# A gelu that writes back into its PSUM bank, and a reordered opening, in a fused linear-attention and mixer-MLP kernel

## The chip, the core and the metric

The kernel runs on one core of one Trainium2 chip. The metric is the device time of one execution in microseconds (us), and lower is better. The five engines are named as in the profile: PE (matrix multiply; PEld is its weight load), DVE (vector), ACT (scalar, activations), POOL (GpSimd) and SP, whose queue issues nearly all DMAs.

## What is computed

The reference, cut to what matters. The sequence has S = 2048 tokens, the model width is D = 640, the hidden width F = 1728, and there are 32 heads of 20.

```python
xn = layernorm(x)
q, k, v = split_heads(xn @ wqkv)
pq, pk = q @ w_phi, k @ w_phi                      # per head
phi_q = concat([softmax(pq), softmax(-pq)])        # the feature maps
phi_k = concat([softmax(pk), softmax(-pk)])
o = (phi_q @ (phi_k.T @ v)) / (phi_q @ phi_k.T @ 1 + 1e-6)
h = gelu(layernorm(xn) @ w1 + b1)                  # the channel-mixing MLP
out = x + o @ wo + (h @ w2 + b2)
```

## The kernel before, in words

Float32 products are made from exact splits: `split` writes a rounded copy `hi` (ACT, L61) and the rest `lo` (a subtraction on DVE or POOL, L64), and `mm3` (L70 to L72) adds three products, hi by hi, hi by lo and lo by hi. Tokens stand in four blocks of 512 (b = 0 to 3), F in 14 chunks of 128 (c), taken in pairs (group g, member j). Model width is contracted in five steps (kc).

**Order.** In the opening and in the MLP of blocks 0 and 1, instructions of PE, DVE, ACT and POOL stand on their queues in the order in which the code calls them. Steps that run beside the products hang on a generator, `mlp.beside`; `tick()` is called after each `mm3` step and moves that generator to its next `yield`. Between the MLP of blocks 0 and 1 and the second half of the kernel only PE's order is the code's; DVE, ACT, POOL and, throughout, SP's DMA queue are ordered by the scheduler when the program is built. An engine runs its queue strictly in order, and so does SP.

**Opening.** PE runs 18 warm-up products (L579). `stats` (L138 to L162) makes each token's mean and scale, `centre` (L166) and `scale` (L170, L172) normalise token tiles x0[0] to x0[3] in place, one on DVE and one on ACT of each pair. `make_y0` (L174) transposes a pair of tiles on PE (L181) into PSUM banks, in pieces of 2, 2 and 1 of the five kc blocks, and `split` turns each piece into y[0] hi (ACT) and lo (DVE). `half_first` (L542) then makes the hidden products of chunks 0 and 1 for that half of the tokens (30 products of 256 columns, L549). PSUM tiles come from `Banks`, which hands out the eight banks by the list given to it; `pall` is the list of the opening. The gelu of these four results (`zs`) is called later, from `next_y` (L652).

**First pass and second pass of the MLP.** `Mlp.first` (L273) makes a hidden product of 128 by 512 in a bank of `self.ph` (banks 0, 1, 2 in turn) and calls `Mlp.gelu` (L281): ACT reads the bank, adds the bias and writes gelu to the SBUF tile `gt` (L286), ACT copies `gt` to hi, DVE subtracts for lo. So the bank is free again as soon as ACT has read it. `passes` (L289) calls `first` for j = 0 and 1 and then makes five second products m = 0 to 4 in banks 5, 6, 7 (`self.po`), each added to the accumulator by DVE (L329, L331). A hidden tile of (g, j, b) = (0, 0, 2) is first copied to `gt` by DVE (L284).

**`next_y`** runs beside group 0 and 1 of block 0: `rows` (L187) sends means and scales through a PE transpose (L197) and DRAM and back as a broadcast tile `m` (L202, L207); the gelu of `zs`; the splits of the w2 halves of chunks 2 and 3 (`parts[c][1]()`: ACT copy, POOL subtraction); after four ticks the subtraction on the feature maps' weights `wpt` (L669, DVE), which products L646 read later; nine ticks on, normalising block 1 into y[1] (L677 POOL, L679 DVE, L681 ACT, L683 DVE).

**The join in the middle.** After the attention projections (L906, L976) come the first passes of group 0 for blocks 2 and 3: first product (0,2) j = 0 and j = 1, the last key-value product (L976, L980), then (0,3) j = 0 and j = 1, at 431 to 446 us. `mlp.ph` is there the same turn of banks 0, 1, 2 as the projections use. At this time DVE transposes the last query features (L1003), SP stores them (L1009: sixteen DMAs of 160 KB), loads t-combinations of y into y[3] (L1345: four DMAs of 256 KB), weights (L354, L356) and the first features back for the attention (L1176, L1178). The products of `cross` (L395) read these y[3] tiles.

Of the kernel before, what the change touches and what calls it, by code (L numbers as in the profile page):

```python
# [10 lines left out]
AF = mybir.ActivationFunctionType  # L11
# [4 lines left out]
P = 128  # L16
# [35 lines left out]
def tile_kernel(ctx: ExitStack, tc: tile.TileContext, x, xT, wkT, wqT, wv, wphi, wo, w1, b1, w2, b2,  # L52
# [4 lines left out]
    def split(hi, lo, src, scale=None, eng=nc.vector, first=nc.scalar):  # L57

        if scale is None:
            if first is nc.scalar:  # L60
                nc.scalar.activation(hi, src, AF.Copy)  # L61
            else:
                first.tensor_copy(hi, src)
            eng.tensor_tensor(lo, src, f(hi), op=ALU.subtract)  # L64
        else:
            nc.scalar.activation(hi, src, AF.Copy, scale=scale)
            nc.vector.scalar_tensor_tensor(lo, src, scale, f(hi), op0=ALU.mult, op1=ALU.subtract)
# [100 lines left out]
    def scale(t, xb, act=False):  # L168
        if act:
            nc.scalar.activation(xb, xb, AF.Copy, scale=ry[:, t:t + 1])  # L170
        else:
            nc.vector.tensor_scalar_mul(xb, xb, ry[:, t:t + 1])  # L172

    def make_y0(half, xbs, ptile):  # L174

        cols = slice(half * 256, half * 256 + 256)
        for c0, n in ((0, 2), (2, 2), (4, 1)):
            ps = ptile()
            for c in range(n):
                for i in range(2):  # L180
                    nc.tensor.transpose(ps[:, c * 256 + i * P:c * 256 + (i + 1) * P],  # L181
                                        xbs[i][:, (c0 + c) * P:(c0 + c + 1) * P], idt)
            src = ps[:, :n * 256].rearrange("p (c t) -> p c t", c=n)
            cs = slice(c0, c0 + n)
            split(y[0][0][:, cs, cols], y[0][1][:, cs, cols], src)
            yield
# [27 lines left out]
    class Mlp:  # L214
# [67 lines left out]
        def gelu(self, g, j, pz, gt, hh, hl, out=False):  # L282
            if out:
                nc.vector.tensor_copy(gt, pz)  # L284
                pz = gt
            nc.scalar.activation(gt, pz, AF.Gelu_apprx_tanh, bias=b1t[:, 2 * g + j:2 * g + j + 1])  # L286
            split(hh, hl, gt)

        def passes(self, g, b, ws, hid=None):  # L289

# [243 lines left out]
    nc.scalar.dma_start(b1t, b1)  # L534
    nc.scalar.dma_start(b2t, b2)
    y[0], y[1] = ([yp.tile([P, KC, 512], F32R, name=f"y{p}{b}") for p in range(2)] for b in range(2))
    gts = mtile(4)
    hid = [mtile(2 * j + 1, F32R) for j in range(2)]
    hid = [(h[:, 0, :512], h[:, 1, :512]) for h in hid]
    pall = Banks(5, 6, 7, 3, 4, 0, 1, 5, 2, 6)  # L540
# [1 line left out]
    def half_first(half, *order):  # L542

        cols = slice(half * 256, half * 256 + 256)
        pz = [pall()[:, cols] for _ in range(2)]
        last = {op[0]: op for op in order}
        for j, wi, yi in order:
            for kc in range(KC):
                nc.tensor.matmul(pz[j], wc[j][wi][:, kc, :], y[0][yi][:, kc, cols],  # L549
                                 start=(wi, yi, kc) == (0, 0, 0), stop=kc == KC - 1 and last[j] == (j, wi, yi))  # L550
        return [lambda j=j: mlp.gelu(0, j, pz[j], *[m[:, cols] for m in (gts[:, j, :512], *hid[j])]) for j in range(2)]

    x1 = load_x(range(4, 8), xp)
    for c, pool in ((2, None), (3, r0)):
# [27 lines left out]
    centre(0, x0[0])  # L582
    step(s01, 3)
    centre(1, x0[1])
    scale(0, x0[0])
    scale(1, x0[1], True)
    parts[0][0]()
    step(s23, 2)
    y01, y23 = make_y0(0, x0[:2], pall), make_y0(1, x0[2:], pall)
# [3 lines left out]
    step(s23, 1)  # L593
    centre(2, x0[2])
    centre(3, x0[3])
    scale(2, x0[2])
    scale(3, x0[3], True)
    zs = half_first(0, *((j, wi, yi) for j in range(2) for wi, yi in ((0, 0), (1 - j, j), (j, 1 - j))))
    parts[2][0]()
    step(s47, 2)  # L600
    step(y23, 4)
    zs += half_first(1, *((j, wi, yi) for ops in (((0, 0), (1, 0)), ((0, 1),)) for j in range(2) for wi, yi in ops))
    parts[3][0]()
    step(s47, 2)
    step(s01, 1)
    step(s47, 1)
    step(s47, 1)
    rows1 = rows(1, 1, xp, Banks(3), 1, nc.scalar)
    next(rows1)
    for c in range(2):  # L610
        parts[c][1](nc.vector)
# [41 lines left out]
    def next_y():  # L653

        for _ in range(3):
            yield
        next(rows1)
        for z in zs[:2]:
            z()
        finish(rows1)  # L660
        mr = load_rows(1)
        first_raws.extend(raws(jobs[0]))
        for z in zs[2:]:
            z()
        for c in range(2, 4):
            parts[c][1]()
        for _ in range(4):
            yield
        nc.vector.tensor_tensor(wpt[:, :, :, 1:], wpt[:, :, :, 1:], wpt[:, :, :, 0:1].to_broadcast([G6, 6, 6, DF]), op=ALU.subtract)  # L669
        for _ in range(9):  # L670
            yield
        xcs = {}
        for n in range(2 * KC + 5):
            c, i = divmod(n, 2)
            if i == 0 and c < KC:
                xcs[c] = xp.tile([P, D], F32, name="xb")[:, :512]
                nc.gpsimd.tensor_tensor(xcs[c], acc[1][:, c], mr[:, 0], op=ALU.subtract)  # L677
            if i == 0 and 0 <= (d := c - 1) < KC:
                nc.vector.tensor_tensor(xcs[d], xcs[d], mr[:, 1], op=ALU.mult)  # L679
            if i == 1 and 0 <= (d := c - 1) < KC:  # L680
                nc.scalar.activation(y[1][0][:, d], xcs[d], AF.Copy)  # L681
            if i == 0 and 0 <= (d := c - 2) < KC:
                nc.vector.tensor_tensor(y[1][1][:, d], xcs[d], f(y[1][0][:, d]), op=ALU.subtract)  # L683
            yield
        for st in (s23, s47):
            step(st, 1)
            yield
# [924 lines left out]
```

## Time and profile before

| | before |
|---|---|
| runs, us | 709.28, 710.75, 711.32; median 710.75 |
| the profiled execution, us | 709.75 |
| its span, us | 708.0 |
| PE busy | 701.1 (99%) |
| DVE, ACT, POOL busy | 526.4, 353.1, 435.6 |
| granted PE clock | 0.999 |
| DMA moved | 107.61 MB, mean 152 GB/s |

A row of the timeline has start, duration (both us), engine, line, operation, out<-in, form and count; in brackets the idle time before it and what ended it. The list of waits has engine, tile and line, what was waited for, then total us, times and longest us. Rows of a tile give the shortest, median and longest duration in ns. "SPq" is an issue on SP's queue: its duration is the issue, not the transfer.

### The profile page before, as it was taken

The numbers are of one execution on the slowest core, as the hardware profiler recorded it, in microseconds if no ns is written. First come the engines' busy times: TensorE is split into PE (matmuls) and PEld (weight loads), VectorE is DVE, ScalarE is ACT, GpSimd is POOL, SyncE is SP. The second block draws the span as 40 slices with busy tenths as digits, with TensorE's granted clock in tenths as the row PEclk, the third lists the DMA queues.
The fourth block names the chain that finished last, engine by engine and source line by source line (L and its number), as shares of the span: only waits on it lengthen the run. The fifth ranks groups of instructions, "written<-read, shape, count | busy, mean of one in ns | idle before, by whom it ended". The sixth has DMA issues, their size and how long they took to land.

```text
span 708.0 us, 9794 instructions
## 1 busy us (share of the span) xinstructions
PE 701.1 (99%) x3369; PEld 590.3 (83%) x3369; DVE 526.4 (74%) x840; ACT 353.1 (50%) x583; POOL 435.6 (62%) x374
## 2 busy tenths in 40 slices
PE   9999999999999999999999999999999999999998
PEld 7788888888888888888888888878888878888886
DVE  7877755988745788788888878748678785696773
ACT  6434554444434545544444547457676757561250
POOL 3611314577245997898777979548688897462530
PEclk9999999999999999999999999999999999999999
DMA  9823642475621227336400708873355558537212
GB/s 328 287 74 113 190 122 98 156 263 174 219 105 74 94 75 231 86 97 200 114 0 15 177 0 316 227 215 126 109 160 172 164 166 276 216 124 262 91 60 104
DMA packets 66295, 107.61 MB, mean 152 GB/s; under 512 B 7478, under 2 KB 31830, under 8 KB 64366
## 3 DMA queue, kind: packets, MB, share of 16 engines
q1 hardware_dynamic: 65942, 106.98, 47.1%
q8 instruction: 26, 0.43, 0.2%
q14 instruction: 23, 0.19, 0.1%
q10 hardware_dynamic: 304, 0.01, 0.0%
HBM read 72.42 MB, written 34.55 MB: 151 GB/s over the span
## 4 chain that ended last, share of the span: by engine, by line
PE 93%; DVE 4%; ACT 1%; DMA 1%; issue 0%; ACTq 0%; DVEq 0%; SPq 0%
PE bank L906 28%; PE bank L70 18%; PE bank L72 18%; PE bank L71 18%; PE bank L976 3%; PE bank L646 2%; PE bank L1214 1%; PE bank L1215 1%; DVE st L138 1%; DMA e<-e 1%; PE bank L308 1%; PE bank L327 1%; PE bank L326 1%; PE bank L307 1%; PE bank L1146 1%
## 5 line engine op out<-in xcount | busy, mean ns | idle before, releaser
L906 PE MATMUL bank<-wkh,y 128*128 128x512 f32 (+1 forms) x480 | 139.6, 365 | 0.0
L64 POOL TENSOR_TENSOR w<-r,w 128x640 fp32r<-128x640 f32 x32 | 52.3, 1648 | 93.1 <-ACT w L61 57.7
L70 PE MATMUL bank<-m,w 128*128 128x512 f32 x274 | 108.0, 394 | 1.1 <-DVE acc L329 1.0
L71 PE MATMUL bank<-m,w 128*128 128x512 f32 x274 | 106.8, 390 | 0.0
L70 PE MATMUL bank<-y,w 128*128 128x512 f32 (+1 forms) x274 | 106.5, 389 | 0.0
L71 PE MATMUL bank<-y,w 128*128 128x512 f32 (+1 forms) x274 | 106.1, 387 | 0.0
L72 PE MATMUL bank<-y,w 128*128 128x512 f32 (+1 forms) x270 | 104.4, 387 | 0.0
L72 PE MATMUL bank<-m,w 128*128 128x512 f32 x262 | 102.1, 390 | 0.0
L906 PEld LDWEIGHTS bank<-wkh,y 128*128 128x128 f32 x480 | 87.6, 188 | 13.2
L906 PE MATMUL bank<-wkl,y 128*128 128x512 f32 (+1 forms) x240 | 87.4, 364 | 0.0
L942 ACT ACTIVATE m<-m,rs_all 128x1280 f32<-128x1280 f32 x32 | 43.7, 1365 | 42.9 <-POOL m L941 42.8
L70 PEld LDWEIGHTS bank<-m,w 128*128 128x128 f32 x274 | 51.5, 188 | 12.4 <-DVE acc L329 1.4
L70 PEld LDWEIGHTS bank<-y,w 128*128 128x128 f32 x274 | 51.5, 188 | 10.8 <-issue 0.4
L71 PEld LDWEIGHTS bank<-y,w 128*128 128x128 f32 x274 | 51.5, 188 | 10.5 <-DMA y<-t 0.4
L71 PEld LDWEIGHTS bank<-m,w 128*128 128x128 f32 x274 | 51.5, 188 | 10.4 <-DVE m L461 0.2
L72 PEld LDWEIGHTS bank<-y,w 128*128 128x128 f32 x270 | 50.8, 188 | 10.3
L944 DVE TENSOR_REDUCE sm<-m 128x64 f32<-128x1280 f32 x32 | 47.4, 1482 | 14.9 <-ACT m L942 14.8
L72 PEld LDWEIGHTS bank<-m,w 128*128 128x128 f32 x262 | 49.2, 188 | 10.3
L906 PE MATMUL bank<-w,y 128*128 128x512 f32 x240 | 57.4, 391 | 0.0
L941 POOL TENSOR_TENSOR m<-m,mx 128x640 f32<-128x640 f32 (+2 forms) x48 | 44.4, 938 | 19.3 <-DVE mx L930 19.3
L331 DVE TENSOR_TENSOR acc<-bank,acc 128x512 f32<-128x512 f32 x70 | 47.0, 684 | 11.0 <-PE bank L72 6.1
L64 DVE TENSOR_TENSOR m<-m,m 128x512 fp32r<-128x512 f32 (+1 forms) x34 | 27.9, 828 | 36.0 <-ACT m L61 36.0
(216 smaller groups left out, 1516.7 us busy)
## 6 DMA issues: line engine op xcount, KB each, us to landing
r<-in_w SPq DMA_DIRECT2D x52, 320.0 KB
e<-e SPq DMA_DIRECT2D x40, 256.0 KB
e<-acc SPq DMA_DIRECT2D x52, 160.0 KB
acc<-in_xT SPq DMA_DIRECT2D x4, 1280.0 KB
t<-t SPq DMA_DIRECT2D x8, 512.0 KB
tf<-t SPq DMA_DIRECT2D x2, 1536.0 KB
xb<-in_x SPq DMA_DIRECT2D x8, 320.0 KB
t<-in_x SPq DMA_DIRECT2D x8, 320.0 KB
```

Source lines behind the costliest of these rows:

```text
L64: eng.tensor_tensor(lo, src, f(hi), op=ALU.subtract)
L70: nc.tensor.matmul(ps, lh, rh, start=first, stop=False, **kw)
L71: nc.tensor.matmul(ps, lh, rl, start=False, stop=False, **kw)
L72: nc.tensor.matmul(ps, ll, rh, start=False, stop=last, **kw)
L138: nc.vector.bn_stats(st[:, i, h, :], xb[:, h * 320:(h + 1) * 320])
L331: nc.vector.tensor_tensor(acc[b][:, m, :], pw, acc[b][:, m, :], op=ALU.add)
L646: nc.tensor.matmul(ps[:, u * nh * DF:(u + 1) * nh * DF], raw[:nh * DH, u * P:(u + 1) * P], wpt[:nh * DH, g, :nh, 1:], start=True, stop=True)
L906: nc.tensor.matmul(ps, lh[:, kc, c], rh[:, kc], start=n == 0, stop=n == 3 * KC - 1)
L941: subs[n, t] = nc.gpsimd.tensor_tensor(ep[:, s], a, b, op=ALU.subtract)
L942: exps[n, t] = nc.scalar.activation(e, e, AF.Exp, scale=rs_all[:, t:t + 1])
L944: nc.vector.tensor_reduce(sm, e.rearrange("p s (h f) -> p (s h) f", f=DH), axis=AX, op=ALU.add)
L976: nc.tensor.matmul(kvp[g // 2][:, (g % 2) * 240:(g % 2) * 240 + 240].rearrange("p (s f) -> p s f", s=4), v[:, g * VS:(g + 1) * VS], ft[:, ...
```

## The change

It has five parts.

1. `Mlp.gelu` writes gelu back into the PSUM bank (`pz`), and both parts of the split read it there. `gt` stays in use for (0, 0, 2), where `pz` is `gt`, and for (6, 1). The opening's `gts` tile goes.
2. `scale_pair`: the second tile of a pair is scaled on ACT for its first three kc blocks and on DVE for the last two.
3. `make_y0` transposes and splits in pieces of 1, 2, 2 blocks.
4. The second `half_first` runs over kc outside, chunks and weight parts inside. The first keeps its order. `rows1` takes bank 7 in place of bank 3.
5. In `next_y` the w2 half of chunk 2 gets its hi from DVE, the `wpt` subtraction follows at once, and chunk 3's w2 half comes seven ticks later; the total of ticks is unchanged.

```diff
+    def scale_pair(t):
+        scale(t, x0[t])
+        scale(t + 1, x0[t + 1][:, :3 * P], True)
+        scale(t + 1, x0[t + 1][:, 3 * P:])
+
     def make_y0(half, xbs, ptile):
-        for c0, n in ((0, 2), (2, 2), (4, 1)):
+        for c0, n in ((0, 1), (1, 2), (3, 2)):
...
-            nc.scalar.activation(gt, pz, AF.Gelu_apprx_tanh, bias=b1t[:, 2 * g + j:2 * g + j + 1])
-            split(hh, hl, gt)
+            nc.scalar.activation(pz, pz, AF.Gelu_apprx_tanh, bias=b1t[:, 2 * g + j:2 * g + j + 1])
+            split(hh, hl, pz)
...
-        for j, wi, yi in order:
-            for kc in range(KC):
-                nc.tensor.matmul(pz[j], wc[j][wi][:, kc, :], y[0][yi][:, kc, cols],
-                                 start=(wi, yi, kc) == (0, 0, 0), stop=kc == KC - 1 and last[j] == (j, wi, yi))
+        for op in order:
+            j, wi, yi, kc = op
+            nc.tensor.matmul(pz[j], wc[j][wi][:, kc, :], y[0][yi][:, kc, cols], start=(wi, yi, kc) == (0, 0, 0), stop=last[j] == op)
...
-    scale(0, x0[0])
-    scale(1, x0[1], True)
+    scale_pair(0)
...
-    scale(2, x0[2])
-    scale(3, x0[3], True)
-    zs = half_first(0, *((j, wi, yi) for j in range(2) for wi, yi in ((0, 0), (1 - j, j), (j, 1 - j))))
+    scale_pair(2)
+    zs = half_first(0, *((j, wi, yi, kc) for j in range(2) for wi, yi in ((0, 0), (1 - j, j), (j, 1 - j)) for kc in range(KC)))
...
-    zs += half_first(1, *((j, wi, yi) for ops in (((0, 0), (1, 0)), ((0, 1),)) for j in range(2) for wi, yi in ops))
+    zs += half_first(1, *((j, wi, 0, kc) for kc in range(KC) for j in range(2) for wi in range(2)),
+                     *((j, 0, 1, kc) for j in range(2) for kc in range(KC)))
...
-    rows1 = rows(1, 1, xp, Banks(3), 1, nc.scalar)
+    rows1 = rows(1, 1, xp, Banks(7), 1, nc.scalar)
...
-        for c in range(2, 4):
-            parts[c][1]()
-        for _ in range(4):
-            yield
+        parts[2][1](nc.vector)
         nc.vector.tensor_tensor(wpt[:, :, :, 1:], wpt[:, :, :, 1:], wpt[:, :, :, 0:1].to_broadcast([G6, 6, 6, DF]), op=ALU.subtract)
-        for _ in range(9):
+        for _ in range(7):
+            yield
+        parts[3][1]()
+        for _ in range(6):
             yield
```

Three places show what this does to the queues. Line numbers of the changed kernel are 2 to 5 higher.

**DVE in the opening**, from the rows' copy to the first second-pass addition. Before (`m` are SBUF tiles of the hidden layer, `w` weights, `bank` PSUM):

```order
L199 COPY sr_406<-bank_404 8x128
L64 TENSOR_TENSOR m_150<-m_149,m_150 128x256
L64 TENSOR_TENSOR m_151<-m_149,m_151 128x256
L64 TENSOR_TENSOR m_150<-m_149,m_150 128x256
L64 TENSOR_TENSOR m_151<-m_149,m_151 128x256
L64 TENSOR_TENSOR m_390<-m_389,m_390 128x512
L669 TENSOR_TENSOR wpt<-wpt 120x36x19
L64 TENSOR_TENSOR m_438<-m_389,m_438 128x512
L329 SCALAR_TENSOR_TENSOR acc_103<-bank_459,b2t,acc_103 128x512
```

The same stretch of DVE in the changed kernel:

```order
L204 COPY sr_407<-bank_405 8x128
L64 TENSOR_TENSOR m_149<-bank_265,m_149 128x256
L64 TENSOR_TENSOR m_150<-bank_266,m_150 128x256
L64 TENSOR_TENSOR m_149<-bank_325,m_149 128x256
L64 TENSOR_TENSOR m_150<-bank_326,m_150 128x256
L63 CAST w_173<-r_160 128x640
L668 TENSOR_TENSOR wpt<-wpt 120x36x19
L64 TENSOR_TENSOR m_391<-bank_392,m_391 128x512
L64 TENSOR_TENSOR m_438<-bank_439,m_438 128x512
L334 SCALAR_TENSOR_TENSOR acc_103<-bank_458,b2t,acc_103 128x512
```

The `wpt` subtraction moved ahead of both 512-column subtractions, the w2 copy of chunk 2 is new on DVE, and each L64 has now one operand in PSUM.

**DVE at the join in the middle**, around the subtraction for the hidden tile (0,2) j = 1, `m3`. Before:

```order
L1003 STREAM_TRANSPOSE acc1_2045<-m1_3995 128x10x32 x2
L1003 STREAM_TRANSPOSE et_2046<-m1_3995 128x10x32
L1003 STREAM_TRANSPOSE acc0_2044<-m1_3995 128x10x32
L64 TENSOR_TENSOR m3_4161<-m4_4139,m3_4161 128x512
L1119 COPY kxs_4204<-kxa_2031 123x160
```

And in the changed kernel, with the bank's number in the name (`bank2`):

```order
L1005 STREAM_TRANSPOSE acc1_2046<-m1_3996 128x10x32 x2
L1005 STREAM_TRANSPOSE et_2047<-m1_3996 128x10x32
L1005 STREAM_TRANSPOSE acc0_2045<-m1_3996 128x10x32
L64 TENSOR_TENSOR m3_4162<-bank2_4163,m3_4162 128x512
L1121 COPY kxs_4205<-kxa_2032 123x160
```

No row moved; the subtraction now reads bank 2 itself. The next user of bank 2 on PE's queue is the first product of (0,3) j = 1, `bank2_4241` (`bank2_4240` before).

**SP's queue at the join.** Before, from the weights' load to the first feature load (`e_73` is the store of the features of block 3, `y` the tiles of y[3], `t` the combinations in DRAM):

```order
L356 DMA r_4112<-in_w 128x640
L1345 DMA y_3061<-t_86 128x512
L1345 DMA y_3060<-t_86 128x512
L1009 DMA e_73<-acc_2045 32x10x128 x8
L1009 DMA e_73<-et 32x10x128 x4
L1009 DMA e_73<-acc_2044 32x10x128 x4
L1345 DMA y_3060<-t_87 128x512
L1345 DMA y_3061<-t_87 128x512
L354 DMA r_4367<-in_w 128x640
L354 DMA r_4368<-in_w 128x640
L1176 DMA e<-e_70 80x512
```

The changed kernel:

```order
L361 DMA r_4113<-in_w 128x640
L1011 DMA e_73<-acc_2046 32x10x128 x8
L1011 DMA e_73<-et 32x10x128 x4
L1011 DMA e_73<-acc_2045 32x10x128 x4
L1347 DMA y_3061<-t_86 128x512
L1347 DMA y_3062<-t_86 128x512
L1347 DMA y_3061<-t_87 128x512
L1347 DMA y_3062<-t_87 128x512
L359 DMA r_4368<-in_w 128x640
L359 DMA r_4369<-in_w 128x640
L1178 DMA e<-e_70 80x512
```

The first two y loads moved from ahead of the sixteen feature stores to behind them. Apart from the operands, ACT's queue differs at the join by one swap (the first copy L392 of the next weights now stands ahead of the hi copy of (0,3) j = 1) and in the opening by the w2 copies named above; POOL's queue has the same rows in the same order.

## Prediction on record

> **What bounds the kernel now.** I read the page first, then the list of waits of PE's weight loads, then the timelines of the places that it names.
>
> ```profile
> span 708.0 us, 9794 instructions
> ...
> PE   9999999999999999999999999999999999999998
> ...
> PEclk9999999999999999999999999999999999999999
> ```
>
> PE is busy in every slice at full clock. The change alters no product of PE, so it can only move PE's idle time. Because the ends of matmuls are modelled, the idle time is read from the weight loads; these rows hold most of it beside the start, which is not touched (waited-for us in total, times, longest):
>
> ```profile
> PEld bank L70 <- DVE acc L329: 1.4, 1, 1.4
> ...
> PEld bank L549 <- ACT y L61: 0.9, 4, 0.3
> PEld bank L70 <- ACT m L449: 0.7, 1, 0.7
> ...
> PEld bank L71 <- DMA y<-t: 0.4, 1, 0.4
> ```
>
> The waits for L329 and for y at L549 are what the opening's parts can take away, and the last two lie behind the join in the middle. Everything that the change could win lies in about 2.5 us, 0.35% of the time; what it could lose is not bounded by this list.
>
> **The opening, first term.** The weight loads of the opening, then ACT:
>
> ```profile
> 9.64 0.30 PEld L549 LDWEIGHTS bank<-y,w 128*128 128x128 f32 x2 [0.27 <-ACT y L61]
> 10.13 3.45 PEld L549 LDWEIGHTS bank<-y,w 128*128 128x128 f32 x28 [0.19 <-ACT y L61]
> 13.83 1.17 PEld L181 LDWEIGHTS bank<-idt,xb 128*128 128x128 f32 x10 [0.25 <-issue]
> 15.26 0.30 PEld L549 LDWEIGHTS bank<-y,w 128*128 128x128 f32 x2 [0.27 <-ACT y L61]
> 15.75 3.45 PEld L549 LDWEIGHTS bank<-y,w 128*128 128x128 f32 x28 [0.19 <-ACT y L61]
> ```
>
> ```profile
> 7.29 0.83 ACT L170 ACTIVATE xb<-xb,ry 128x640 f32<-128x640 f32 x1 [0.17 <-DVE ry L158]
> 8.99 1.36 ACT L61 ACTIVATE y<-bank 128x512 fp32r<-128x512 f32 x3 [0.24 <-PE bank L181]
> ```
>
> 28 loads in 3.45 us are 0.123 us each, so a kc block lasts 0.123 us in the first half, where ACT makes one in about 0.27 (1.36 / 5). The first half keeps its order and stays bound by ACT's five blocks. In the second half four products use one block, 0.49 us, so ACT keeps ahead, and the first piece is one block, ready before the ten transposes end: 0.27 + 0.19 = **0.46 us** go. Ahead of it, ACT scales 384 columns in place of 640: at most 0.83 x 256/640 = 0.33 us less, at least nothing; I take 0.2, since short instructions cost more per column. DVE pays with one more scaling, and then this pair decides:
>
> ```profile
> 11.50 1.16 DVE L153 TENSOR_TENSOR rr<-rr,q 128x4 f32<-128x4 f32 x1
> ```
>
> ```profile
> 11.06 1.58 POOL L64 TENSOR_TENSOR w<-r,w 128x640 fp32r<-128x640 f32 x1
> ```
>
> DVE's tiny product ended at 12.66, POOL's subtraction at 12.64: DVE was held by POOL, which started after ACT's copy. So ACT's 0.2 us come through to the scaling of tiles 2 and 3, and the second half starts 0.2 us sooner (of the 0.25 idle at 13.83). The extra DVE scaling is hidden in that hold; if the hold were gone it would cost its 0.2 to 0.3 us. First term: 0.66 us, between 0.2 and 0.9.
>
> **The opening, second term.** The wait for L329:
>
> ```profile
> 27.45 1.89 DVE L64 TENSOR_TENSOR m<-m,m 128x512 fp32r<-128x512 f32 x1 [1.62 <-ACT m L61]
> 29.27 0.86 DVE L669 TENSOR_TENSOR wpt<-wpt 120x684 f32<-120x684 f32 x1
> 30.05 0.68 DVE L64 TENSOR_TENSOR m<-m,m 128x512 fp32r<-128x512 f32 x1
> 30.65 2.05 DVE L329 SCALAR_TENSOR_TENSOR acc<-bank,b2t,acc 128x512 f32<-128x512 f32 x3
> ```
>
> ```profile
> 30.08 0.39 PE L72 MATMUL bank<-m,w 128*128 128x512 f32 x1
> 31.45 0.50 PE L70 MATMUL bank<-m,w 128*128 128x512 f32 x1 [0.98 <-DVE acc L329]
> ```
>
> ```profile
> 24.51 0.42 ACT L61 ACTIVATE m<-m 128x256 fp32r<-128x256 f32 x1
> 24.83 1.35 ACT L61 ACTIVATE w<-r 128x640 fp32r<-128x640 f32 x2
> ```
>
> ```profile
> 20.84 0.89 DVE L63 CAST w<-r 128x640 fp32r<-128x640 f32 x2
> ```
>
> PE's step is 0.23 us here, so L70 was due at 30.31 and lost 1.14. The chain behind it is the L64 of 1.89 us (the same form takes 0.68 two rows on; POOL was subtracting weights beside the long one), then `wpt`, then the next L64. In the changed kernel the last short hi copy still ends at 24.93; DVE's subtraction for it (0.4) and the new cast (0.45) bring `wpt` to 25.8, with chunk 2's copy gone from ACT and chunk 3's later. `wpt` ends at 26.66. ACT, without the 1.35 us, makes both gelus and hi copies (some 0.65 each) by 27.4, the second gelu being ready to start when its product ends near 25.5. So the first L64 runs at 26.6, the second at 27.4 to 28.1, and the first L329 ends at 28.7; PE wants the bank at 30.31 - 0.66 = 29.65. 1.14 us go, with 0.95 to spare.
>
> What PSUM as source costs is seen in two rows of the subtraction's line (ns, shortest, median, longest):
>
> ```profile
> L64 DVE TENSOR_TENSOR m<-m,m x34: 412/693/1891, 22.5 to 628.1; 128x512 fp32r<-128x512 f32 x30, 128x256 fp32r<-128x256 f32 x4
> L64 DVE TENSOR_TENSOR y<-bank,y x6: 416/637/682, 9.7 to 16.8; 128x512 fp32r<-128x512 f32 x4, 128x256 fp32r<-128x256 f32 x2
> ```
>
> The form with a bank is no longer, and never reached 1.89. [...]
>
> **What is late next** is the normalising of block 1:
>
> ```profile
> 30.70 7.19 POOL L677 TENSOR_TENSOR xb<-acc,m 128x512 f32<-128x512 f32 x5 [1.91 <-DMA m<-r]
> ```
>
> ```profile
> 38.36 0.68 DVE L331 TENSOR_TENSOR acc<-bank,acc 128x512 f32<-128x512 f32 x1
> ```
>
> ```profile
> 39.20 0.47 PE L70 MATMUL bank<-m,w 128*128 128x512 f32 x1
> ```
>
> POOL's start hangs on a DMA round trip that the change doesn't shorten (ACT issues it after the table load at the same time), and DVE's normalising steps wait for POOL block by block. PE, 1.8 us ahead, is due at 37.40 in the bank that L331 frees. By DVE's order L331 moves only from 38.36 to about 37.0 and ends near 37.7, so about 0.35 us come back (nothing to 0.6). The opening wins 0.66 + 1.14 - 0.35 = **1.45 us**, between 0.8 and 2.1.
>
> Between 43 and 431 us the other engines wait for PE, and PE for almost nothing; I carry the gain through and cost the PSUM gelu there at nothing, since three banks turn and a bank is wanted again, at the soonest, two products (30 steps of 0.23 us, 6.8 us) after its own ended.
>
> **The join: a wait added.** There this cover is missing, because the key-value product takes one of the three banks. (0,2) j = 1 and (0,3) j = 1 both have bank 2.
>
> ```profile
> 442.75 0.39 PE L70 MATMUL bank<-y,w 128*128 128x512 f32 x1
> ```
>
> ```profile
> 442.43 0.64 ACT L61 ACTIVATE m<-m 128x512 fp32r<-128x512 f32 x1
> ```
>
> ```profile
> 443.49 0.89 DVE L1003 STREAM_TRANSPOSE acc<-m 128x320 f32<-128x320 f32 x2
> ...
> 445.09 0.64 DVE L64 TENSOR_TENSOR m<-m,m 128x512 fp32r<-128x512 f32 x1
> ```
>
> PE began (0,3) j = 1 at 442.75; the gelu had read the bank by then. Now the bank is free only when DVE's subtraction ends, which stands behind four transposes on DVE: 445.73. The wait costs 445.80 - 442.75 = **3.05 us**. Behind this matmul queue all of PE's later products; DVE's transposes don't depend on them. If DVE came to the subtraction right after the hi copy (443.07), the wait would be 1.0: those are the ends.
>
> **And SP.** The y loads now follow the sixteen stores:
>
> ```profile
> 446.33 5.20 SPq L1009 DMA_DIRECT2D e<-acc  x8
> ...
> 458.59 1.44 SPq L1345 DMA_DIRECT2D y<-t  x2
> ...
> 461.38 0.36 SPq L1176 DMA_DIRECT2D e<-e  x1
> ```
>
> ```profile
> 463.94 0.19 PEld L71 LDWEIGHTS bank<-y,w 128*128 128x128 f32 x1 [0.38 <-DMA y<-t]
> ...
> 469.04 0.19 PEld L70 LDWEIGHTS bank<-tf,w 128*128 128x128 f32 x1 [0.70 <-ACT m L449]
> ```
>
> ```profile
> DMA packets 1043, 2.00 MB, mean 266 GB/s; under 512 B 127, under 2 KB 138, under 8 KB 1042
> ```
>
> The last row is of 460.4 to 467.9 us, with the DMA engines busy throughout. Two more loads, 0.52 MB, ahead of the fourth y and of the first features take 0.52 / 266 GB/s = 2.0 us. PE already waited there, 0.38 for y and 0.70 behind a feature load (ACT's copy L449 stood behind it). PE comes 3.05 late: it needs y at 463.56 + 3.05 = 466.6, and y lands at 465.9, so the 0.38 go; the features let it on at 469.04 + 2.0 = 471.0, and PE is there at 469.04 - 0.70 - 0.38 + 3.05 = 471.0. The two losses overlap: 3.05 - 0.38 - 0.70 = 1.97, and by the DMAs 2.0. I take **2.0 us**, between 1.5 (1.0 of bank wait, DMAs faster) and 3.05 (nothing overlaps).
>
> **Sum.** -1.45 + 2.0 = +0.55 us. The profiled execution took 709.75, 1.0 less than the median of the runs, 710.75; it becomes 710.3, and the median **711.3**. From the terms' bounds, -0.6 to +2.3.
>
> **Rivals.**
> *The loss doesn't overlap: slower.* The feature loads come later than 471.0, the point from which they decide. For it: the sixteen stores, 2.6 MB, were issued in the 12.3 us from 446.33 to 458.59; at that rate the 0.52 MB take 2.5 us, and SP's two more issues (1.44 by the row of 458.59) come ahead of L1176, of which I add 1.1, the rest lying beside the transfers: 3.6. Net 3.6 - 1.45 = +2.15: 712.9, and more with an opening that wins less. Against it: the y rows are longer than the stores' and ran at 266.
> *The bank wait is short: faster.* DVE takes the subtraction early (wait 1.0) and the loads run in the idle DMA time: loss 0.5, opening 2.0: 709.25.
> *The opening gives back.* `wpt` and POOL's subtraction for chunk 2 become ready together near 25.8; if POOL goes first, DVE is held as in the 1.89 us row, L329 ends at 30.1 and 0.6 us come back: 711.9. [...]
> *It doesn't do what it says*: the waits for y at L549 stay, since ACT and not the order sets them: +0.46, 711.8.
>
> **Chances.** The forecast 0.5, slower 0.2, faster 0.13, the two last together 0.17. The range, 709.4 to 713.3, reaches from the short bank wait to just beyond the slower rival and includes the spread of the runs. A measurement of this kernel tells about 0.3% (2.1 us) from no change. Only the slower rival crosses it on that side (0.2), and for the other side hardly 2 us are to be had: 0.05; within it, 0.75.
>
> **What would show it.** In the changed profile: no 0.27 and 0.19 in the second half of L549, and L70 following 30 x 0.123 = 3.7 us after the transposes' end; no wait for L329 near 30; PE 1.2 to 1.7 us ahead at the first product of block 1 (42.95 before); one PE wait of about 3 us on DVE m L64 near 441; no wait for y<-t; at 475 us a lag of about 0.5 us. I am wrong if that bank wait is missing, or if the lag there is under -0.6 or over 2.3.

## The result, and the profile after

| | before | changed |
|---|---|---|
| median of the runs beside each other, us | 710.12 (709.28 to 711.32) | 713.10 (711.92 to 714.34) |
| ratio, 95% interval | | 1.0038 (1.0026 to 1.0051) |
| the profiled execution, us | 709.75 | 711.92 |
| its span, us | 708.0 | 710.1 |

The change costs 2.7 us, from 1.8 to 3.6 by the interval. The forecast was +0.55 us (711.3), with a range up to 713.3: the time lies inside, near its upper end, and the loss is a little over the 0.3% that a measurement of this kernel can tell from no change (the six runs of before spread over 0.29%). The profiled executions differ by 2.17 us. In the groups further below two executions, of 773.76 us (granted clock 0.851) and of 3448.28 us, lie far from all others and are left out of ratios and counts.

The page of the changed kernel, in the same slices as before (1/40 of the span each, 17.75 us):

```profile
span 710.1 us, 9795 instructions
...
PE   8999999999999999999999999899999999999998
...
PEclk9999999999999999999999999999999999999999
```

Two digits of PE fell to 8. In the first slice the weight loads of the warm-up products were done sooner (5.31 us in place of 6.78) and PE stood 1.35 us for the first tile, with no loss: its transposes began at 7.96 (8.13 before). The other slice, from 444 to 461.5 us, is the join. The waits of PE's weight loads say for what (total us, times, longest):

```profile
PEld bank L70 <- DVE m L64: 3.3, 1, 3.3
...
PEld bank L70 <- DVE acc L334: 1.1, 1, 1.1
PEld bank L70 <- DVE acc L336: 0.9, 2, 0.8
...
PEld bank L553 <- ACT y L61: 0.5, 2, 0.3
...
PEld bank L553 <- DVE y L64: 0.3, 1, 0.3
```

The first row is new and longer than all that the opening lost before. The two waits for L329 (now L334) and for y at L549 (now L553) only shrank, and one for L336 came up. To see when time was won and lost I paired each PE product with the same one of before and took the difference of their starts ("PE's offset", minus means ahead):

| product that before began at, us | 16.5 | 31.6 | 43 | 442 | 447 | 475 | last, 708 |
|---|---|---|---|---|---|---|---|
| offset of the changed kernel, us | -0.64 | -0.98 | -0.12 | -0.02 | +3.16 | +2.33 | +2.17 |

**Opening.** PE's weight loads of the second half, after the transposes:

```profile
13.78 1.12 PEld L186 LDWEIGHTS bank<-idt,xb 128*128 128x128 f32 x10
14.87 3.69 PEld L553 LDWEIGHTS bank<-y,w 128*128 128x128 f32 x30
```

Thirty loads in one row without a bracket: PE waits for no block of y. But then DVE:

```profile
27.68 0.87 DVE L668 TENSOR_TENSOR wpt<-wpt 120x684 f32<-120x684 f32 x1 [2.10 <-DMA wpt<-in_wphi]
28.47 1.28 DVE L64 TENSOR_TENSOR m<-bank,m 128x512 fp32r<-128x512 f32 x2
```

The 1.89 us subtraction of before is gone (two take 1.28), but DVE stood 2.10 us for the load of `wpt`, with both of them queued behind. And the normalising of block 1, on POOL, began 1.19 us later than before (31.89 against 30.70):

```profile
31.89 1.29 POOL L679 TENSOR_TENSOR xb<-acc,m 128x512 f32<-128x512 f32 x1 [1.91 <-DMA m<-r]
```

What PE felt of the two, at the first and the fourth second-pass group:

```profile
30.46 0.50 PE L70 MATMUL bank<-m,w 128*128 128x512 f32 x1 [0.64 <-DVE acc L334]
...
39.04 0.50 PE L70 MATMUL bank<-m,w 128*128 128x512 f32 x1 [0.57 <-DVE acc L336]
```

These stood at 31.45 and 39.20 before: the lead goes from 0.99 to 0.16.

**Join.** PE, then DVE:

```profile
442.50 0.39 PE L72 MATMUL bank<-y,w 128*128 128x512 f32 x1
445.78 0.50 PE L70 MATMUL bank<-y,w 128*128 128x512 f32 x1 [2.89 <-DVE m L64]
```

```profile
443.48 0.89 DVE L1005 STREAM_TRANSPOSE acc<-m 128x320 f32<-128x320 f32 x2
444.30 0.46 DVE L1005 STREAM_TRANSPOSE et<-m 128x320 f32<-128x320 f32 x1
444.69 0.46 DVE L1005 STREAM_TRANSPOSE acc<-m 128x320 f32<-128x320 f32 x1
445.08 0.65 DVE L64 TENSOR_TENSOR m<-bank,m 128x512 fp32r<-128x512 f32 x1
```

The four transposes stand ahead of the subtraction that frees the bank, and PE starts as it ends: 445.78, forecast 445.80. SP, and ACT at the first feature tile:

```profile
457.56 2.43 SPq L1347 DMA_DIRECT2D y<-t  x4
...
461.32 0.36 SPq L1178 DMA_DIRECT2D e<-e  x1
```

```profile
468.20 0.63 ACT L1209 ACTIVATE m<-e 128x512 fp32r<-128x512 f32 x1
```

ACT no longer waits for the features, and PE's waits for y (0.38) and behind L449 (0.70) are gone: PE is so late that both are there. So the offset falls by 0.83, from +3.16 to +2.33.

### The profile page after: what moved, and what is told of

It is laid out like the page before. It is cut to its first block, busy times and chain, and to the rows that moved or that the text cites. A ratio compares the mean times of both kernels' runs of the same rounds, so it can differ in the third digit from the quotient of the medians.

```text
span 710.1 us, 9795 instructions
## 1 busy us (share of the span) xinstructions
PE 699.4 (98%) x3369; PEld 589.0 (83%) x3369; DVE 522.2 (74%) x843; ACT 350.3 (49%) x582; POOL 434.7 (61%) x374
## 4 chain that ended last, share of the span: by engine, by line
PE 85%; DVE 6%; POOL 3%; DMA 2%; ACT 2%; issue 1%; SPq 0%; POOLq 0%; DVEq 0%
PE bank L908 23%; PE bank L70 18%; PE bank L71 17%; PE bank L72 17%; PE bank L978 2%; PE bank L648 2%; POOL m L943 2%; PE bank L1216 1%; PE bank L1217 1%; DVE st L138 1%; POOL m L954 1%; DMA m<-r 1%; DMA r<-sr 1%; PE bank L312 1%; PE bank L331 1%
## 5 line engine op out<-in xcount | busy, mean ns | idle before, releaser
L64 POOL TENSOR_TENSOR w<-r,w 128x640 fp32r<-128x640 f32 x32 | 52.7, 1659 | 93.8 <-ACT w L61 63.5
L336 DVE TENSOR_TENSOR acc<-bank,acc 128x512 f32<-128x512 f32 x70 | 47.2, 684 | 12.2 <-PE bank L72 6.9
L908 PEld LDWEIGHTS bank<-w,y 128*128 128x128 f32 x240 | 44.4, 188 | 8.5
```

The costliest lines, as they stand in the source:

```text
L336: nc.vector.tensor_tensor(acc[b][:, m, :], pw, acc[b][:, m, :], op=ALU.add)
L908: nc.tensor.matmul(ps, lh[:, kc, c], rh[:, kc], start=n == 0, stop=n == 3 * KC - 1)
```

## The experiments

All comparisons stand beside runs of the kernel before in the same group. Offsets are those of the profiled execution; POOL is the start of the first subtraction of block 1.

| kernel | median, us | ratio (95%) | at 31.6 | at 43 | at 442 | at 475 | wait at the join | POOL |
|---|---|---|---|---|---|---|---|---|
| changed | 713.10 | 1.0038 (1.0026 to 1.0051) | -0.98 | -0.12 | -0.02 | +2.33 | 3.3 | 31.89 |
| changed, again | 713.83 | 1.0057 (1.0041 to 1.0074) | -0.93 | +0.02 | +0.42 | +4.24 | 3.3 | 32.06 |
| gelu in PSUM only | 712.86 | 1.0047 (1.0034 to 1.0059) | -0.62 | -0.62 | +0.46 | +2.83 | 3.3 | 31.25 |
| bank 0 at the join | 709.27 | 0.9998 (0.9987 to 1.0009) | -1.59 | -1.07 | -1.06 | -0.89 | 1.1 | 30.94 |
| SBUF gelu at the join | 708.64 | 0.9981 (0.9973 to 0.9990) | -1.32 | -1.17 | -1.17 | -1.19 | none | 30.84 |
| the same, again | 708.52 | 0.9984 (0.9976 to 0.9993) | -1.67 | -0.71 | -0.45 | -1.28 | none | 31.31 |
| opening only | 709.22 | 0.9991 (0.9982 to 1.0000) | -0.86 | -0.78 | +0.06 | -0.30 | none | 31.25 |
| opening's order only | 710.20 | 1.0003 (0.9992 to 1.0013) | -0.03 | -0.01 | +0.85 | +0.06 | none | 31.82 |
| sooner subtraction only | 710.34 | 1.0010 (0.9995 to 1.0024) | -1.02 | -0.95 | +0.16 | -0.67 | none | 31.09 |
| rows in two halves | 708.67 | 0.9970 (0.9958 to 0.9983) | -1.44 | -1.35 | -1.22 | -1.48 | none | 30.67 |
| wpt later | 708.25 | 0.9964 (0.9950 to 0.9977) | -1.39 | -0.26 | -0.26 | +0.07 | none | 31.16 |
| both of these | 708.76 | 0.9967 (0.9953 to 0.9981) | -2.14 | -1.56 | -1.01 | -1.83 | none | 29.83 |
| y behind the stores | 709.93 | 0.9993 (0.9979 to 1.0007) | +0.54 | +2.14 | +3.24 | +4.68 | y | 31.05 |

### SBUF gelu at the join

```diff
-            self.gelu(g, j, pz, gt, hh, hl, (g, j, b) == (0, 0, 2))
+            self.gelu(g, j, pz, gt, hh, hl, (g, j, b) == (0, 0, 2), g == 0 and b > 1)
...
-        def gelu(self, g, j, pz, gt, hh, hl, out=False):
+        def gelu(self, g, j, pz, gt, hh, hl, out=False, sbuf=False):
...
+            to = gt if sbuf else pz
...
-            split(hh, hl, pz)
+            split(hh, hl, to)
```

In the lines between, the gelu's activation writes to `to` in place of `pz`.

> The changed kernel, with the gelu of first passes of group 0, blocks 2 and 3, again going through SBUF (so bank 2 is free when the gelu has read it); the opening and every other first pass stay as changed. The order of the queues then puts the two y loads ahead of the sixteen feature stores again on SP, as before the change. Bank theory (the 3.03 us wait at 445.78, less the 0.8 us of older waits that it covers, is the loss): the wait for DVE L64 at 445 us is gone, PE's products around 475 us start 0.2 to 0.9 us earlier than in the kernel before, and the time is 0.2 to 1.0 us below before. Rival, gelu in PSUM costs in the steady state: still 1 to 2.5 us above before. Rival, SP order (the y loads behind the stores are the loss, the bank wait is only where PE would have stood anyway): also at or below before, so this run alone doesn't tell it from the bank.

The wait for DVE is gone. All that its PE waits for between 455 and 476 us is this (the list of waits of that stretch):

```profile
PEld bank L71 <- DMA y<-t: 0.9, 1, 0.9
```

PE stands at 475 us where it stood at 442. The time is 1.35 us below before, a little more than the 0.2 to 1.0 that I expected, and 4.1 us below the changed one by the two ratios. The whole loss of the change thus goes away with three gelus out of all those that moved to PSUM: the edit names four, but the one of (0, 0, 2) went through `gt` in the changed kernel too.

### Gelu in PSUM only

The kernel before with part 1 and bank 7 for `rows1`.

> The kernel before, with the gelu written back into its PSUM bank and the normalising's products in bank 7, nothing else of the change. Bank theory: the same 3 us wait for DVE L64 at 445 to 446 us, offsets of PE against before near 0 until 442 us and +2.3 us at 475 us, and a time 2.0 to 2.8 us above before. Rival, the opening's new order is what costs: within 0.5 us of before. Rival, gelu in PSUM costs in the steady state: PE falls behind already between 50 and 440 us, by 0.5 us or more.

The wait is there without any change of the opening (PE's timeline):

```profile
446.28 0.50 PE L70 MATMUL bank<-y,w 128*128 128x512 f32 x1 [2.90 <-DVE m L64]
```

From 442 to 475 us PE loses 2.37 us, to the changed kernel's 2.35. The time is 3.3 us above before (2.4 to 4.2), where I expected 2.0 to 2.8; the section on the two controls gives a likely reason. The opening is no part of that. A stall at 193 us (PE for DVE's second-pass sum, 1.2 us) also shows between 43 and 442 us, but several kernels without PSUM gelus lose there too (opening only, 0.84 us; order only, 0.86; sooner subtraction only, 1.11), and with PSUM gelus throughout the changed kernel loses 0.10 and 0.40 and that with bank 0 0.01, so it doesn't speak for a steady cost, though by its number (1.08 us) the sign of that rival was there.

### Opening only

The changed kernel with every gelu through SBUF.

> The changed kernel with every gelu going through SBUF again: the change of the opening alone (order of products, finer transposes, subtractions sooner). Theory of the opening (it wins 1 us by 31 us and gives most of it back at 39 us, where block 1's normalising waits for the rows' round trip through DRAM): PE at 43 us 0.1 to 0.6 us ahead of before, the same to the end, time 0 to 0.7 us below before. Rival, the opening's order itself costs: time 0.5 to 2 us above before. Rival, the prediction's own working of the opening (no wait beyond 0.35 us at the second block): 1.45 us below before.

-0.64 us (-1.3 to 0). No harm from the new order, and no 1.45 us either. PE is 0.78 us ahead at 43 us and has lost that lead by 442 us.

### Bank 0 at the join

```diff
+    mlp.ph = Banks(1, 0, 2)
     this = mlp.passes(0, 3, ws)
```

> The changed kernel, all gelus in PSUM, but the second product of the fourth block's first pass takes bank 0 in place of bank 2 (the three banks of the first passes are started at another place there). Bank 0 is free once the last sums of keys are added, some 2 us sooner than bank 2. Bank theory: PE's wait at 445 us shrinks from 3.3 to 0.5 to 1.5 us, PE at 475 us stands within 0.3 us of before or up to 0.9 us ahead, time 0 to 0.9 us below before. Rival, gelu in PSUM costs by itself at the join, whatever the bank (PE waits as long for the next evacuation in place of this): 1.5 to 2.7 us above before.

The same products, the same gelus in PSUM, another bank:

```profile
442.56 0.50 PE L70 MATMUL bank<-y,w 128*128 128x512 f32 x1 [0.71 <-DVE kxa L987]
```

PE now waits for the sum of keys that frees bank 0, and 1.0 us in place of 3.2 is lost between 442 and 447 us. The time is that of before. So the long wait comes from which bank the next product takes, and not from writing the gelu to PSUM as such. SP's order in this kernel is that of before, as it is in the one with SBUF gelus at the join: the two runs do not yet separate the bank from SP.

### y behind the stores

SBUF gelus at the join, and the four y loads made to follow the last store:

```diff
-            nc.sync.dma_start(f(y[3][p][:, 2 * q]), t_dram[q][:, 0, p])
+            with tc.issue_after(stores[-1]):
+                nc.sync.dma_start(f(y[3][p][:, 2 * q]), t_dram[q][:, 0, p])
```

> The kernel with SBUF gelus at the join, but with all four y loads behind the sixteen feature stores on SP, which is the order of the changed kernel. Bank theory: the SP order costs nothing, PE at 475 us stands where it stands at 442 us or up to 0.5 us better, time within 0.4 us of the kernel with SBUF gelus at the join. The prediction's own SP term: features and y 0.5 to 2.0 us later, PE at 475 us 0.5 to 2 us worse than at 442 us.

Here my bank theory was wrong in a part. PE's waits from 455 to 476 us:

```profile
PEld bank L71 <- DMA y<-t: 1.1, 2, 0.6
PEld bank L70 <- ACT m L455: 0.9, 1, 0.9
PEld bank L70 <- DMA y<-t: 0.4, 1, 0.4
PEld bank L70 <- issue: 0.3, 1, 0.3
```

From 442 to 475 us PE loses 1.44 us, where the same kernel with the old order of SP loses none. By the ratios the order costs 0.6 to 0.9 us against the two groups of that kernel, with intervals that overlap, so it is the profile that shows it, more than the time. SP's order has the price that the prediction gave it (0.5 to 2); in the changed kernel no wait for y is left, since the bank holds PE back longer than y is late. No run has the bank wait with the old order of SP, so the two prices are not measured apart in the changed kernel itself. (The opening of this profile is off, and its lag of 2.14 us at 43 us comes from there; the last section comes back to it.)

### Opening's order only, and sooner subtraction only

The kernel before with parts 2 to 4, and the kernel before with part 5; both with SBUF gelus.

> The kernel before with only the finer transposes and the two halves' products by contraction chunk. Theory: PE waits nowhere in the second half's products and is 0.35 to 0.8 us ahead of before at 16.5 us; the wait of 1.4 us for L329 at 30 us stays, and because DVE's subtractions there did not move, PE at 43 us is 0 to 0.6 us ahead. Time 0 to 0.6 us below before. Rival, the lead at 16.5 us comes from elsewhere (the warm-up): the waits for ACT and DVE in the second half stay and the lead is under 0.2 us.

> The kernel before with only the sooner subtraction in the feature maps and the two weight chunks' splits around it. Theory: PE at 16.5 us within 0.2 us of before, the wait for L329 at 30 us shrinks from 1.4 us to 0.7 to 1.1 us (DVE now waits for the wpt load instead), PE at 31.6 us is 0.3 to 0.7 us ahead and at 43 us 0 to 0.7 us, by where POOL's first subtraction falls (plus 7.17 us). Time within 0.5 us of before. Rival, the subtraction itself was the cost: the wait goes and PE at 31.6 us is 1.1 us or more ahead.

At 16.5 us the order alone is 0.77 us ahead and the subtraction alone 0.11, as expected. Then the waits of each, first the order alone, second the subtraction alone:

```profile
PEld bank L70 <- DVE acc L334: 2.1, 1, 2.1
```

```profile
PEld bank L549 <- ACT y L61: 0.9, 4, 0.3
PEld bank L70 <- DVE acc L329: 0.5, 1, 0.5
```

The order's lead runs straight into the wait for DVE's sum, which grows from 1.4 to 2.1 us: alone it is worth nothing. The subtraction shortens that wait by 0.9 us, more than I expected, with the y waits as before, and its lead of 1.02 us at 31.6 is above the 0.3 to 0.7 of the theory. Both times are within 0.3% of before.

### Rows in two halves, wpt later, both

Three versions of the kernel with SBUF gelus at the join. The first loads block 1's means and scales with two DMAs, the second puts DVE's subtraction on `wpt` behind the third sum L335, the third does both:

```diff
+            for a in range(2):
+                loads[b] = nc.sync.dma_start(mr[:, a], row[:, a * 512:a * 512 + 512].to_broadcast([P, 4 * P])).ins
...
         parts[2][1](nc.vector)
-        nc.vector.tensor_tensor(wpt[:, :, :, 1:], ...)
         for _ in range(7):
             yield
         parts[3][1]()
         for _ in range(6):
             yield
+        nc.vector.tensor_tensor(wpt[:, :, :, 1:], ...)
```

> The kernel with SBUF gelus at the join, whose one load of block 1's two rows to all partitions (m<-r, 512 KB) is split into two: the means first, then the reciprocal deviations, which POOL's subtraction doesn't need. Theory of the round trip (in the five profiles of the opening as changed or of before, PE's product at the fourth group of block 1 starts 7.17 us after POOL's first subtraction wherever POOL was late; POOL waits for that load): POOL's first subtraction starts at 29.6 to 30.2 us instead of 30.84 to 31.9, and PE at 39 us stands as far ahead as at 31 us, 1.2 to 1.6 us ahead of before; time 0 to 0.4 us below the kernel with SBUF gelus at the join. [...] Rival, landing depends on the backlog of the first loads alone: POOL's start stays at 30.8 to 31.9.

> The kernel with SBUF gelus at the join, with DVE's subtraction in the feature maps (wpt) moved behind the third of the sums L335, so that its wait for the wpt load stands ahead of nothing that PE needs early. Theory: the PE wait for L335 at 30 us (0.85 to 1.1 us in the runs so far) goes, and PE at 31.6 us is 1.8 to 2.3 us ahead of before in place of 1.0 to 1.6; at 39 us it is back at POOL's first subtraction plus 7.17 us (1.2 us ahead of before if POOL starts at 30.84), so that the time is within 0.3 us of the kernel with SBUF gelus at the join. Rival, the PE wait at 30 us is set by ACT and the products, not by wpt: PE at 31.6 us stays 1.0 to 1.6 us ahead.

> Both edits together: rows loaded in two halves, wpt subtracted behind the third sum. Theory: both waits go and PE at 43 us is 1.7 to 2.3 us ahead of before; time 0.3 to 1.0 us below the kernel with SBUF gelus at the join, 1.5 to 2.3 us below before, unless a later wait for a transfer (ACT for t at 184 us) takes back what is over 0.6 us, as it did in two of the profiles. Rival: either edit alone does as much as both.

POOL's row with the halves alone, then with both edits:

```profile
30.67 2.55 POOL L684 TENSOR_TENSOR xb<-acc,m 128x512 f32<-128x512 f32 x2 [1.16 <-DMA m<-r]
```

```profile
29.83 6.58 POOL L686 TENSOR_TENSOR xb<-acc,m 128x512 f32<-128x512 f32 x4 [0.70 <-DMA m<-r]
```

From SP's issue of the load to that start went 4.1 to 5.1 us in the twelve profiles with one load, and 3.9 and 3.6 us with two: with half the bytes POOL follows the issue sooner. In the first kernel it starts hardly sooner for that, at 30.67 (30.70 to 32.06 with one load), and not at the 29.6 to 30.2 that I expected. Its PE keeps 1.35 of the 1.44 us at 43 us: nearly no give-back. With `wpt` later, the wait for the sum at 30 us is 0.2 us (alone) and none (both); the lead at 31.6 us, with both, is 2.14 us, the largest of all. Alone it does not show at 31.6, since that profile was 0.11 us behind before already at 8.4 us, where the others are 0.4 to 0.7 ahead; counted from 8.4 us it gains 1.50 by 31.6, as the kernel with both does (1.51). With both edits 1.56 us are left at 43 us, a little under the 1.7 to 2.3 of the theory.

In time nothing more is measured: the three medians lie within 0.51 us and their intervals overlap that of the kernel they start from. What PE keeps at 43 us is not what the time keeps (see the column at 442).

### The two controls

> The kernel with SBUF gelus at the join once more, beside the others of this group. Bank theory: 1 to 2 us below before, 3 to 4.5 us below the changed kernel in the same group; PE at 475 us stands where it stands at 442 us, within 0.6 us.

> The changed kernel a second time. Bank theory: the wait for DVE L64 at 445 us is there again with 3.2 to 3.4 us, and PE falls back by 2.2 to 2.6 us between 442 and 475 us. In the opening PE at 43 us is 0.1 to 1.2 us ahead of before, at POOL's first subtraction plus 7.17 us. Time 1.5 to 3 us above before. Rival, the first profile was a chance draw: the wait differs by over 0.5 us.

The SBUF gelus at the join again: 1.1 us below before (0.5 to 1.7), as expected, and 5.3 us below the changed kernel, more than the 3 to 4.5 expected; PE gains 0.83 us between 442 and 475 us, where I expected 0.6 at most. The changed kernel again: the same wait of 3.3 us, but PE fell back by 3.82 us, where the first profile had 2.35 and I expected 2.2 to 2.6. The reason is in the row of windows (from:to, its length, PE busy, granted clock, DMA share, GB/s) of this second profile,

```profile
442.50:446.20 3.70, 0.83 (x4) 0.97 0.67 267
446.20:449.20 3.00, 2.99 (x7) 0.50 0.52 91
```

against the first one:

```profile
446.20:449.20 3.00, 3.00 (x15) 1.00 0.64 113
```

After the wait PE ran at half clock for 3 us: 7 products in place of 15. How often this happens is read, with less certainty, from the mean granted clock of each timed run (3 us at half clock make a mean of 0.998 over 710 us, by estimate): of the changed kernel's twelve, four had 1.0 (mean 712.3 us) and eight 0.995 to 0.998 (mean 714.0); of the 81 executions of before in the last three groups, none was under 0.999. Of the kernel with the PSUM gelu only, four of five were; of the 106 runs of the kernels without the long wait, six. So the wait has a second price, 1.7 us in two runs of three, which accounts for the medians losing 2.7 and 4.0 us where the first profile, at full clock, lost 2.17. Only one of the eight runs was profiled; where the others lost their clock, and why two of them are as low as 0.995, no trace shows.

## Why the prediction came out as it did

The place and the direction were right, and the size of two terms was not. That the time lies in the range is partly luck. The terms' own bounds ended at +2.3, and the range went on to 713.3, which is +2.55 from the 710.75 that I started from, to take in a rival whose mechanism did not occur and the spread of the runs; the loss is 2.7, and the time is inside only because the kernel before ran at 710.12 beside it. From +0.55 to the +2.17 of the profile, the opening accounts for 1.33 us, the join for 0.35 and the stretch between for 0.10, less 0.16 after 475 us; the rest, to +2.7, is the clock.

- **First term of the opening (0.66 us): right in most profiles.** 0.64 at 16.5 us in the changed kernel, 0.77 with the order alone, and no wait left in the second half; the two kernels that keep the old order are 0.05 and 0.11 ahead. ACT's scaling of 384 columns took 0.61 and 0.62 us, where 640 took 0.83 (1.6 ns a column against 1.3): the 0.2 less that I took. Over the 11 profiles with the new order it is 0.56 in the mean, but from 0.88 ahead to 0.12 behind: the second profile of the changed kernel is the one behind, since DVE there waited 0.67 us for a load of x, and PE for DVE, in the first half.
- **Second term (1.14 us): the step that failed.** "DVE's subtraction for it (0.4) and the new cast (0.45) bring `wpt` to 25.8." I counted what stands ahead on DVE's queue and not the transfer: before, the instruction ran at 29.27 without a wait for its load, so no row showed when that landed. At its new place it waits for the load until 27.68, with both subtractions behind it, and 1.1 us of wait for L334 stay; in the ten profiles in which DVE waits for the load, it starts at 26.85 to 28.69. The profile before had a hint: from 22 us on, its DMA rate by microsecond was 382, 272, 132, 32 and 17 GB/s, and `wpt` was the last load that SP issued ahead of that (13.39), so by estimate it landed near the end of that backlog. Moving the subtraction later took the wait down to 0.2 us or none: 2.14 us of lead at 31.6 with both edits, where 1.8 were forecast.
- **Give-back (0.35 us, "nothing to 0.6"): its mechanism right, its size wrong.** I took POOL's start for fixed at 30.70. It hangs on a round trip through DRAM, and over the 12 profiles with one load it falls anywhere from 30.70 to 32.06; the profile that I worked from was the earliest draw of them. In eight of the 14 profiles PE's product of 39.20 starts 7.14 to 7.17 us after POOL; 31.89 + 7.15 = 39.04 in the changed kernel. So the give-back between 31.6 and 43 us was 0.86 there, 0.95 in its second profile, and 0.15 with SBUF gelus at the join, all three with the same code in the opening. The rival in which POOL goes first and DVE is held did not occur in the changed kernel: its `wpt` took 0.87 and the two L64 0.64 each. It did in three other profiles, where POOL's subtraction began ahead of `wpt`, which then took 1.30 to 1.47 (opening only, sooner subtraction only, y behind the stores).
- **Opening, sum: -1.45 forecast, -0.12 measured**; over the five profiles with the same opening in which `wpt` had landed by 27.73, it is -0.61 in the mean, from -1.17 to +0.02. A sixth, in which it landed at 28.7, stands at +2.14; the last section has it.
- **Steady state at nothing: right.** 0.10 us between 43 and 442 us, 0.40 in the second profile, no more than kernels without PSUM gelus lose there.
- **The bank wait, 3.05 us: right**, since the product that began at 442.75 now began at 445.78, 3.03 later; and shown to be the bank: another bank, 1.1 us; no PSUM gelu at the join, none. That the start too agrees to the hundredths (445.78 for 445.80) is luck: 445.80 was worked out without the opening's lead, which had gone by then.
- **The join's loss, 2.0 us: 2.35 in the profile.** The overlap was right in kind: the bank wait covers SP's order, which alone costs PE 1.44 us. The feature loads were not later than PE, since the stores went out faster (the last group of them ends on SP's queue at 457.46, against 458.48 before), so of the old 0.38 and 0.70 PE won back 0.83.
- **Not in the prediction at all: the clock.** It took PE as running at full clock around the wait; by the mean clocks, in two runs of three it does not.

The rival "the loss doesn't overlap" gave 712.9, near the time, but for another reason: its mechanism, features later than 471.0, was not there (ACT had them at 468.20). Of the signs that I named, the missing waits at L553, the 3 us wait and the missing wait for y came true; the missing wait for L329 and the lead of 1.2 to 1.7 us did not, and the lag at 475 us is 2.33 us, just beyond the 2.3 at which I said I would be wrong.

What stays open is a second loss of the opening's lead, between 145 and 195 us. In seven of the 14 profiles, changed and unchanged openings alike, PE loses 0.4 to 1.1 us there to waits for second-pass sums of DVE; in the others, 0 to 0.3. In six of the seven, ACT's longest wait for a reload from DRAM (`t<-t`) was 4.1 to 5.0 us; in the others it was 1.4 to 3.6, as in the seventh. That points to another transfer, but no experiment took that wait away.

## What to carry to other kernels

A result that is written back into its accumulator bank keeps that bank until its last reader is done: look not at the loop, where banks turn slowly (0.10 and 0.40 us lost here), but at the place where another product takes one from the turn (a wait of 3.3 us here, 1.1 with bank 0), and ask what stands ahead of that reader on its queue. When an instruction is moved ahead of others, what has landed by then counts as much as what is queued (`wpt` held DVE for 2.10 us); a load that was never waited for at the old place says nothing about the new one. A lead that is handed to a chain behind a DRAM round trip is kept only as far as that round trip allows, and a single profile gives one draw of it: POOL's start lies between 30.70 and 32.06 here, and with the same code in the opening 0.12 of 0.98 us of lead were left in one profile and 1.17 of 1.32 in another.

## What the runs showed of the hardware

**After waits of 2.6 and 3.3 us PE ran at a lower clock in two profiles, at 0.67 and 0.50.** Beside the windows above, the profile with y behind the stores had it in its opening. There the load of `wpt` landed late, PE waited 2.58 us for L335, and then (windows as above):

```profile
30.00:34.00 4.00, 2.02 (x7) 0.90 1.03 347
34.00:38.00 4.00, 4.00 (x13) 0.67 0.95 354
```

1.6 us went between 31.6 and 36 us, besides the wait itself. Not every such wait is followed by a lower clock, and its length does not tell which is: at the join PE stood 2.88 us ahead of the window at 0.50, and 2.89 and 2.90 us ahead of windows at 1.00 (the first profile of the changed kernel, and the PSUM gelu only). By the mean clocks it came in eight of the changed kernel's twelve runs; what decides it, no run shows.

Of the six runs under 0.999 among the kernels without the long wait at the join, this is one. All six are of kernels with the sooner `wpt` subtraction (81 runs); the kernels with it at the old place or later (order only, `wpt` later, both) have none in 25. So the other five may be late landings of `wpt` too, but none of them was profiled.

**A near tie between DVE and POOL cost PE 1.2 us in two of the 14 profiles.** In the kernel with SBUF gelus at the join both engines start at 548.82, first DVE, then POOL:

```profile
548.82 0.68 DVE L467 TENSOR_TENSOR m<-m,m 128x512 fp32r<-128x512 f32 x1
```

```profile
548.82 1.84 POOL L1268 TENSOR_TENSOR acc<-acc,rx 128x512 f32<-128x512 f32 x1
```

In the kernel with rows in two halves POOL is 0.01 us ahead, and DVE is the one held:

```profile
548.52 1.82 DVE L471 TENSOR_TENSOR m<-m,m 128x512 fp32r<-128x512 f32 x1
```

```profile
548.51 1.28 POOL L1272 TENSOR_TENSOR acc<-acc,rx 128x512 f32<-128x512 f32 x1
```

PE's lead in that kernel fell there from 1.48 to 0.31 us, though nothing near this place was changed. All 14 profiles have this pair, with starts 0.001 to 0.032 us apart. In 12 DVE is first: it takes 0.68, POOL 1.81 to 1.84, and PE loses 0.05 us at most. In two POOL is first, DVE takes 1.82 or 1.83, and PE loses 1.2 us. The two are the kernels with the largest leads, 1.48 and 1.83, and also the two with the rows in halves; which of these turns the tie was not tested. Either way such a tie can cost most of a lead.
